# Fused attention and MLP: score pieces regrouped across batches, and pairs released earlier

## The chip, the cores and the metric

The kernel runs on one core of a Trainium2 chip. The metric is the device time of one execution in microseconds (us). A core has a matrix engine (PE, which writes its results to PSUM, eight banks of 128 x 512 float32), a vector engine (DVE), an activation engine (ACT), a general engine (POOL) and a queue for transfers (SP). Each engine works through its own list of instructions in order; semaphores make one wait for another. POOL and ACT can issue transfers as well.

## The reference

For 8 batches of 8 heads with 576 tokens and 64 values per head, attention with 16 extra keys in front ("beacons") that every token sees, then an MLP over all 4608 tokens:

```python
k_all = concat([beacon_k, k]); v_all = concat([beacon_v, v])
scores = (q @ k_all.T) / 8                 # causal among the 576, beacons always seen
a = exp(scores - max); a /= a.sum(-1)
x = (a @ v_all) -> 4608 x 512              # heads side by side
h = relu(x @ w_in) ; out = (h * h) @ w_out # 512 -> 2048 -> 512
```

The kernel computes in bfloat16 with float32 sums and leaves out the maximum.

## The kernel before

**Attention.** The heads are taken two at a time: a pair `p` is 4 x batch + 0..3, so there are 32 pairs. The transposed Q and K of a batch lie in `qT` and `kT`, two buffers each, so batch b uses those of batch b - 2. For batches 0 to 2 the transposes are done on PE; for batches 3 to 7 SP loads float32 tiles into `stg`, POOL casts them into `qk_area`, and SP transposes them by DMA into `qT` and `kT` (`add_trans`, line 543).

The causal scores of a pair have 15 blocks of 128 (or fewer) keys by 128 queries. They are packed into four pieces: three of 512 columns and one, the block of keys 0 to 127 with queries 368 to 495, of 128 columns (`WHOLE`, line 724). A piece is a few score matmuls on PE (line 813), with the two heads of the pair in the two halves of the array's rows, into two PSUM banks. One exponential on ACT (line 830) writes a piece into the pair's buffer `pt`, of which there are four. In batches 1 to 7 the fourth pieces of two pairs share two banks (`SHARED`), so a batch has 14 pieces; each pair still has its own exponential of 2 x 128 values for it. Pieces go to PE in **bursts**: a burst is one planned operation that takes all its banks at once. In batches 2 to 7 the 14 pieces make bursts of 3, 3, 3, 3 and 2 (`SIZES`), and every batch begins anew.

When a pair's exponentials are done, DVE masks the diagonal blocks (lines 848 and 852), PE multiplies with V in an AV group of 30 matmuls (line 869), DVE divides by the sums (lines 884 and 885) into `xn`, and, for batches 1 to 7, SP transposes the five tiles of a batch by DMA into `xT` (line 916), once its four pairs are done.

**MLP.** The tokens are taken in nine chunks of 512. A chunk's first stage (line 997) is 16 groups of 4 matmuls into one bank each, which ACT or DVE empty with the relu (lines 1014 and 1016); DVE squares (line 1023). Its second stage (line 1037) is 64 matmuls. Chunk j needs `xT` of the batches that its tokens lie in, and so the last of the four pairs of those batches.

**What sets the order.** A planner, `Order`, runs when the program is built: it keeps a clock with a duration for each operation, gives each engine the ready operation of the lowest priority number, and the result is written out as each engine's fixed list. Score bursts and AV groups come ahead of the MLP. Two things hold a burst back: its banks (bursts may hold six of the eight; the MLP keeps two) and the **gate** of its first pair (line 768): a pair p of batch 1 or later isn't preferred before the MLP's planned PE time has come to 27.7 x (LEAD + PACE x (p - 4)) us, with 27.7 us a chunk, `LEAD` = -0.4 and `PACE` = 0.25 (line 761). When PE has nothing else, the gate is passed over. The planner takes a transfer as arrived at its reckoned landing and a margin, 2.0 us for the transposes into `qT` and `kT`.

Of the kernel before, what the change touches and what calls it, by code (L numbers as in the profile page):

```python
# [319 lines left out]
def kernel(  # L320
# [29 lines left out]
    def sb(name, shape, dt):  # L350
        return pool.tile(shape, dt, name=name)
# [16 lines left out]
          for i in range(2)]  # L368
    ks = [qk_area[0:NP, (2 * i + 1) * WS:(2 * i + 2) * WS].rearrange("p (h s d) -> p h s d", h=H, s=NS)
          for i in range(2)]  # L370
    bks = sb("bks", [128, H, D], BF16)
    spare = {x: sb(f"spare{x}", [NP, NS * 2 * D], BF16) for x in "kq"}
    vb = [sb(f"vb{i}", [128, NT, H, D + 2], BF16) for i in range(2)]
# [13 lines left out]
    def pair(op, k=0):  # L387
        return ps[:, op.held[k]:op.held[k] + 2, :]
# [12 lines left out]
    def wait_for(later, first):  # L401
# [1 line left out]
            mybir.DependencyClass.Sync, mybir.DependencyReason.DATA), reason="order of loads")  # L403

    order = Order(
        pools={"ps": Banks(), "stg": Slots(NSTG), "pt": Slots(NPT)},
        limits={"late": 4, "strip": 6, "av": 4, "mlp": 4, "tp": 6},
        floors={"mlp": 2},
        keep=2,
# [305 lines left out]
    class Phase:  # L715
# [3 lines left out]
        def __init__(self, pieces, diag, last, tiles, off):  # L719
# [31 lines left out]
    ONE_BY_ONE = [[(x, i)] for x in range(HP) for i in range(4)]  # L751
    SHARED = [[(0, 0)], [(0, 1)], [(0, 2)], [(0, 3), (1, 3)], [(1, 0)], [(1, 1)], [(1, 2)], [(2, 0)], [(2, 1)],
              [(2, 2)], [(2, 3), (3, 3)], [(3, 0)], [(3, 1)], [(3, 2)]]
    PIECES = {b: ONE_BY_ONE if b < 1 else SHARED for b in range(B)}
    SIZES = {b: [2] * 7 if b < 2 else [3, 3, 3, 3, 2] for b in range(B)}

    def phases(b):
        return SPLIT if b < NSPLIT else WHOLE

    mlp_chunk_us = 27.7  # L760
    LEAD, PACE = -0.4, 0.25
    norm_ops = {}

    def add_pair(b, pr):
# [20 lines left out]
    def add_scores(pairs, n, sizes, pieces):  # L785

        work = []
        for shared in pieces:
            at, parts = 0, []
            for x, i in shared:  # L790
                parts.append((pairs[x], i, at, phases(pairs[x].b)[n].pieces[i]))
                at += parts[-1][3][2]
            work.append(parts)
        exps = {x.p: [] for x in pairs}
        at = 0
        for size in sizes:
            group = work[at:at + size]
            at += size
            lead = group[0][0][0]
            prio = 100.0 * lead.p + 1000.0 * n + group[0][0][1]  # L800
            every = [part for parts in group for part in parts]
            cols = sum(t1 - t0 for _, _, _, (mms, _, _) in every for _, t0, t1, _ in mms)
            owners = list({x.p: x for x, _, _, _ in every}.values())
            box = {}

            def emit_qk(e, group=group, box=box):
                for k, parts in enumerate(group):
                    st = pair(box["qk"], k)
                    for x, _, lo, (mms, _, _) in parts:
                        for c, t0, t1, col in mms:  # L810
                            for hj in range(2):
                                hp = slice(64 * hj, 64 * hj + 64)
                                nc.tensor.matmul(  # L813
                                    st[:, hj, lo + col:lo + col + t1 - t0],
                                    kT[x.b % 2][hp, x.pr, 128 * c:128 * c + 128],
                                    qT[x.b % 2][hp, x.pr, t0:t1],
                                    start=True, stop=True,
                                )

            qk = add(f"qk{lead.p}.{n}.{group[0][0][1]}", "PE", cols / 2400.0, emit_qk, prio=prio,  # L820
                     deps=[d for x in owners for d in x.qk_deps + [x.take_pt] + early.get((x.b, x.pr, min(n, 1)), [])],
                     take=("ps", "late" if lead.b < NSPLIT and n else "strip", [2] * size), gate=lead.gate, mode="rows")
            box["qk"] = qk
            for x in owners:
                qk_ops[x.p].append(qk)
            for k, parts in enumerate(group):
                own = []
                for x, i, lo, (_, off, width) in parts:
                    def emit_exp(e, off=off, width=width, k=k, x=x, lo=lo, box=box):
                        nc.scalar.activation(pt[x.take_pt.held[0]][:, :, off:off + width],  # L830
                                             pair(box["qk"], k)[:, :, lo:lo + width], AF.Exp, bias=0.0, scale=scale)

                    own.append(add(f"exp{x.p}.{n}.{i}", "ACT", act(2 * width), emit_exp, prio=prio + 0.1 * k,
                                   deps=[qk], give=(qk, k) if len(parts) == 1 else None))
                    exps[x.p].append(own[-1])
                if len(parts) > 1:
                    add(f"share{lead.p}.{n}.{k}", "-", 0.0, None, deps=own, give=(qk, k))
        assert at == len(work)
        for x in pairs:
            add_phase(x.b, x.pr, x.p, n, phases(x.b)[n], x.take_pt, exps[x.p])  # L840

    def add_phase(b, pr, p, n, ph, take_pt, exps):
        base = 100.0 * p + 1000.0 * n
        def emit_mask(e):
            P = pt[take_pt.held[0]]
            at, step, m0, m = ph.diag
            d = P[:, :, at:at + m * step].rearrange("p h (c w) -> p h c w", w=step)[:, :, :, 0:128]
            nc.vector.tensor_tensor(out=d, in0=d,  # L848
                                    in1=tri[:, m0:m0 + m, :][:, None].to_broadcast([128, 2, m, 128]), op=ALU.min)
            if ph.last is not None:  # L850
                d = P[0:LAST, :, ph.last:ph.last + LAST]
                nc.vector.tensor_tensor(out=d, in0=d,  # L852
                                        in1=tri[0:LAST, 1:2, 0:LAST].to_broadcast([LAST, 2, LAST]), op=ALU.min)

        behind = []
        mask = add(f"mask{p}.{n}", "DVE", 0.08 + 0.15 * ph.diag[3] + (0.26 if ph.last else 0.0), emit_mask,
                   prio=base, deps=exps + (tri_ops[:1] if ph is SPLIT[0] else tri_ops), behind=behind)
        tl, nt = ph.tiles, len(ph.tiles)

        def emit_av(e):  # L860
            P = pt[take_pt.held[0]]
            a = pair(av)
            for hj in range(2):
                h = 2 * pr + hj
                for t in tl:
                    for c in range(t + 1):
                        rr = rows_of(c)
                        o = ph.off[c, t]
                        nc.tensor.matmul(  # L869
                            a[:, hj, (t - tl[0]) * (D + 1):(t - tl[0] + 1) * (D + 1)],  # L870
                            P[0:rr, hj, o:o + 128],
                            vb[b % 2][0:rr, c, h, 0:D + 1],
                            start=(c == 0), stop=(c == t),
                        )

        av = add(f"av{p}.{n}", "PE", 0.0585 * sum(t + 1 for t in tl), emit_av, prio=base + (AVP if ph is SPLIT[0] else -150),
                 deps=[mask] + [cast[b, "v", c] for c in range(tl[-1] + 1)] + av_ops[p], take=("ps", "av", [2]),
                 give=take_pt if ph is phases(b)[-1] else None)
        av_ops[p].append(av)

        def emit_norm(e):
            a = pair(av)[:, :, 0:nt * (D + 1)].rearrange("p h (t d) -> p h t d", d=D + 1)
            r = rcp[(2 * p + n) % len(rcp)][:, :, 0:nt]
            nc.vector.reciprocal(r, a[:, :, :, D])  # L884
            nc.vector.tensor_tensor(  # L885
                out=xn[b % 2].rearrange("p t (h d) -> p h t d", d=D)[:, 2 * pr:2 * pr + 2, tl[0]:tl[0] + nt],
                in0=a[:, :, :, 0:D],
                in1=r[:, :, :, None].to_broadcast([128, 2, nt, D]),
                op=ALU.mult,
            )  # L890

        deps = [av]
        if b >= 2:
            deps += [o for (bb, _), o in xt_ops.items() if bb == b - 2]
        norm_ops[p, n] = add(f"norm{p}.{n}", "DVE", 0.25 + 0.148 * nt, emit_norm, prio=base - 150, deps=deps, give=av)
# [215 lines left out]
    for b in range(B):  # L1111
# [21 lines left out]
        if b < NSPLIT:  # L1133
            for x in pairs:
                for n, ph in enumerate(phases(b)):
                    add_scores([x], n, [1] * len(ph.pieces), [[(0, i)] for i in range(len(ph.pieces))])
        else:
            add_scores(pairs, 0, SIZES[b], PIECES[b])
        if b < NXPE:
            add_xt_pe(b)  # L1140
        else:
            add_xt(b)
        for j in range(NCH):
            if min(((j + 1) * TCH - 1) // S, B - 1) == b:
                late.append(j)
        if b >= 1:
            for j in late:
                add_chunk(j)
            late = []

    turns = TURNS.split()
    named = {o.name: o for o in order.ops}
# [42 lines left out]
```

## Time and profile before

| | us |
|---|---|
| median of 3 runs | 337.4 (337.39 to 338.38) |
| the profiled execution's own time | 337.61 |
| its span, from the first to the last instruction | 335.7 |
| PE busy | 326.6 |
| ACT busy | 194.1 |
| DVE busy | 159.9 |

The busy time of an engine is the time in which at least one of its instructions runs. Matmuls overlap in the array, so lengths of single matmuls add up to more than PE's busy time; distances from start to start are read instead. A line number in a row is that of the kernel before. In rows of the timeline the first number is the start in us from the span's start, the second the time to the end of the last instruction of the run of equal ones, and xN their count. A few matmul records are missing from the trace: a row that shows x7 where the code issues 8 can be such a place.

### The profile page before, as it was taken

What the parts mean: (1) busy time and instruction counts of PE and PEld (TensorE: products, weight loads), DVE (VectorE), ACT (ScalarE), POOL (GpSimd) and SP (SyncE); (2) the same over time, 40 slices, a digit from 0 to 9 for tenths busy, and PEclk for the clock granted to TensorE, in tenths of its full rate; (3) what the DMA queues carried; (4) which work ended last, traced back from release to release, by engine and by line L of the source; (5) the groups of instructions that cost most, each with busy time, mean ns of one, the idle gap of its engine ahead of it and who ended that gap; (6) DMA issues with size and microseconds to landing.
All of it is one profiled execution on the core that took longest, in us unless ns stands there. A gap on an engine that the chain in (4) does not pass through costs nothing.

```text
span 335.7 us, 7764 instructions
## 1 busy us (share of the span) xinstructions
PE 326.6 (97%) x3190; PEld 184.3 (55%) x3231; DVE 159.9 (48%) x329; ACT 194.1 (58%) x296; POOL 84.2 (25%) x130
## 2 busy tenths in 40 slices
PE   7899999999999999999999999999999999999996
PEld 5568765554555455545468945554545444444444
DVE  6689985557423762376136812681258303301400
ACT  3887977577465647574566555665576226515611
POOL 8946504513224332223242240420000000000000
PEclk9999999999999999999999999999999999999999
DMA  8999999899979996899799898973110321011003
GB/s 139 173 204 186 200 205 211 143 235 189 226 113 254 236 213 137 204 232 201 133 253 219 180 182 176 209 155 70 64 64 0 63 71 62 2 62 62 2 5 120
DMA packets 144180, 49.17 MB, mean 146 GB/s; under 512 B 130577, under 2 KB 139665, under 8 KB 144145
## 3 DMA queue, kind: packets, MB, share of 16 engines
q1 hardware_dynamic: 125168, 39.63, 58.2%
q0 software_dynamic: 18624, 8.69, 20.1%
q8 instruction: 25, 0.41, 0.5%
q10 hardware_dynamic: 352, 0.36, 0.4%
q14 instruction: 11, 0.08, 0.1%
HBM read 37.22 MB, written 9.44 MB: 139 GB/s over the span
## 4 chain that ended last, share of the span: by engine, by line
PE 91%; POOL 3%; DMA 3%; issue 1%; DVE 1%; ACT 0%; DVEq 0%
PE ps L997 37%; PE ps L1037 36%; PE ps L869 8%; PE ps L813 8%; DMA w_in<-in_moe_w_in_dram 3%; POOL vb L499 1%; PE ps L671 1%; POOL qk_area L635 1%; PE ps L1080 1%; POOL tri L435 0%; DVE g L1016 0%; POOL w_in L958 0%; DVE tri L414 0%; PE ps L933 0%; POOL vb L498 0%
## 5 line engine op out<-in xcount | busy, mean ns | idle before, releaser
L997 PE MATMUL ps<-xT,w_in 128*128 128x512 bf16 (+3 forms) x688 | 133.7, 340 | 1.2 <-DVE g L1016 0.2
L1037 PE MATMUL ps<-w_out,g 128*128 128x512 bf16 x535 | 125.1, 379 | 1.8 <-issue 0.6
L830 ACT ACTIVATE pt<-ps 128x1024 bf16<-128x1024 f32 (+3 forms) x128 | 103.1, 870 | 28.9 <-PE ps L813 27.8
L997 PEld LDWEIGHTS <-w_in 128*128 128x128 bf16 x704 | 65.5, 98 | 55.5 <-issue 4.1
L1014 ACT ACTIVATE g<-ps 128x512 bf16<-128x512 f32 (+2 forms) x111 | 63.3, 570 | 44.1 <-PE ps L997 43.9
L1037 PEld LDWEIGHTS <-g 128*128 128x128 bf16 x560 | 52.2, 98 | 61.7 <-issue 4.0
L1023 DVE TENSOR_TENSOR g<-g 128x1024 bf16<-128x1024 bf16 (+2 forms) x80 | 51.4, 648 | 65.3 <-ACT g L1014 64.8
L450 ACT COPY osb<-ps 128x512 f32<-128x512 f32 (+2 forms) x37 | 21.3, 576 | 56.7 <-PE ps L1037 43.4
L452 POOL CAST qk_area<-stg 128x512 bf16<-128x512 f32 (+2 forms) x50 | 32.7, 659 | 66.1 <-DMA stg<-in_k_dram 33.2
L848 DVE TENSOR_TENSOR pt<-pt,tri 128x1024 bf16<-128x1024 bf16 (+1 forms) x36 | 23.6, 656 | 40.7 <-ACT pt L830 40.7
L869 PEld LDWEIGHTS <-pt 128*128 128x128 bf16 (+1 forms) x960 | 33.7, 97 | 6.6 <-issue 0.6
L452 POOL CAST vb<-stg 128x512 bf16<-128x512 f32 (+1 forms) x30 | 21.9, 734 | 58.9 <-DMA stg<-in_v_dram 52.9
L1016 DVE TENSOR_SCALAR g<-ps 128x512 bf16<-128x512 f32 (+2 forms) x49 | 28.9, 590 | 15.6 <-PE ps L997 15.3
L869 PE MATMUL ps<-vb,pt 128*128 128x65 bf16 (+1 forms) x960 | 35.0, 193 | 0.3 <-DMA vb<-in_v_dram 0.3
L813 PE MATMUL ps<-qT,kT 64*128 64x80 bf16 (+6 forms) x680 | 32.1, 230 | 0.0
L885 DVE TENSOR_TENSOR xn<-ps,rcp 128x640 bf16<-128x640 f32 (+2 forms) x36 | 27.0, 751 | 1.4
L813 PEld LDWEIGHTS <-kT 64*128 64x128 bf16 x680 | 18.2, 95 | 16.3 <-issue 13.5
L884 DVE RECIPROCAL rcp<-ps 128x10 f32<-128x10 f32 (+2 forms) x36 | 7.6, 211 | 32.6 <-PE ps L869 31.5
L450 ACT COPY qT<-ps 128x576 bf16<-128x576 bf16 (+2 forms) x13 | 7.7, 601 | 4.6 <-PE ps L671 3.3
L452 DVE COPY kT<-ps 128x576 bf16<-128x576 bf16 (+2 forms) x13 | 9.0, 706 | 2.6 <-PE ps L671 2.0
L852 DVE TENSOR_TENSOR pt<-pt,tri 80x160 bf16<-80x160 bf16 x32 | 9.8, 308 | 0.0
L499 POOL DMA_DIRECT2D vb<-in_v_dram x10 | 8.5, 851 | 3.5 <-DMA w_in<-in_moe_w_in_dram 3.1
(54 smaller groups left out, 80.8 us busy)
## 6 DMA issues: line engine op xcount, KB each, us to landing
out_dram<-osb SPq DMA_DIRECT2D x17, 512.0 KB, 3.4
stg<-in_q_dram SPq DMA_DIRECT2D x20, 256.0 KB, 4.8
stg<-in_v_dram SPq DMA_DIRECT2D x18, 256.0 KB, 4.7
stg<-in_k_dram SPq DMA_DIRECT2D x15, 256.0 KB, 4.8
w_in<-in_moe_w_in_dram POOLq DMA_DIRECT2D x4, 512.0 KB, 9.6
w_out<-in_moe_w_out_dram POOLq DMA_DIRECT2D x4, 512.0 KB, 9.8
stg<-in_v_dram SPq DMA_DIRECT2D x6, 224.0 KB, 4.5
qk_area<-in_k_dram POOLq DMA_DIRECT2D x4, 288.0 KB, 12.0
```

Of the source, the lines that this page charges most:

```text
L450: nc.scalar.copy(dst, src)
L452: eng[e].tensor_copy(dst, src)
L813: nc.tensor.matmul(st[:, hj, lo + col:lo + col + t1 - t0], kT[x.b % 2][hp, x.pr, 128 * c:128 * c + 128], qT[x.b % 2][hp, x.pr, t0:t1], sta ...
L830: nc.scalar.activation(pt[x.take_pt.held[0]][:, :, off:off + width], pair(box["qk"], k)[:, :, lo:lo + width], AF.Exp, bias=0.0, scale=scale)
L848: nc.vector.tensor_tensor(out=d, in0=d, in1=tri[:, m0:m0 + m, :][:, None].to_broadcast([128, 2, m, 128]), op=ALU.min)
L869: nc.tensor.matmul(a[:, hj, (t - tl[0]) * (D + 1):(t - tl[0] + 1) * (D + 1)], P[0:rr, hj, o:o + 128], vb[b % 2][0:rr, c, h, 0:D + 1], star ...
L885: nc.vector.tensor_tensor(out=xn[b % 2].rearrange("p t (h d) -> p h t d", d=D)[:, 2 * pr:2 * pr + 2, tl[0]:tl[0] + nt], in0=a[:, :, :, 0:D ...
L997: nc.tensor.matmul(h[:, lo - spans[0][0]:hi - spans[0][0]], w_in_sb[:, mc, ft * 128:(ft + 1) * 128], xT[:, mc, lo % RING:lo % RING + hi - lo],
L1014: nc.scalar.activation(dst, h, AF.Relu, bias=0.0, scale=1.0)
L1016: nc.vector.tensor_scalar(out=dst, in0=h, scalar1=0.0, scalar2=None, op0=ALU.max)
L1023: nc.vector.tensor_tensor(out=d, in0=d, in1=d, op=ALU.mult)
L1037: nc.tensor.matmul(o, G[:, fc, ts * 128:(ts + 1) * 128], w_out_sb[:, fc, :], start=(fc == 0), stop=(fc == NFT - 1))
```

## The change

Four things are changed, all in how score pieces are grouped and when they may start.

1. For batches 3 to 7 the fourth pieces of a batch's four pairs go side by side into one piece of 512 columns. One exponential of 128 x 1024 values empties it into a new buffer `rest` (two of them, in a part of `qk_area` that only batch 1 used before), and the AV groups read that block from there. `rest` is held until the four AV groups of the batch are done.
2. The pieces of batches 3 to 7, 13 a batch, go through one list, `flow`: a batch's shared piece first, then the three large pieces of each pair. A burst takes three from its head, whichever batch they are of, and waits for Q, K and the buffers of all pairs in it; what is left of a batch stays for the next one's pieces. At the end two remain and make the last burst.
3. A pair's mask, AV and normalisation, and a batch's `xT` transposes and MLP chunks, are added when its last piece has gone into a burst; their dependences are the same as before.
4. `LEAD` goes from -0.4 to -1.0, for all pairs from batch 1 on.

A dependence of bursts on `early` is dropped, which for the first phase is in the pairs' own list already.

```diff
+    rest = [qk_area[:, 4 * W + 1024 * i:4 * W + 1024 * (i + 1)].rearrange("p (h w) -> p h w", h=2) for i in range(2)]
...
-        pools={"ps": Banks(), "stg": Slots(NSTG), "pt": Slots(NPT)},
+        pools={"ps": Banks(), "stg": Slots(NSTG), "pt": Slots(NPT), "rest": Slots(2)},
...
-    PIECES = {b: ONE_BY_ONE if b < 1 else SHARED for b in range(B)}
-    SIZES = {b: [2] * 7 if b < 2 else [3, 3, 3, 3, 2] for b in range(B)}
+    PIECES = {0: ONE_BY_ONE, 1: SHARED, 2: SHARED}
+    SIZES = {0: [2] * 7, 1: [2] * 7, 2: [3, 3, 3, 3, 2]}
+    FLOW = 3
...
-    LEAD, PACE = -0.4, 0.25
+    LEAD, PACE = -1.0, 0.25
...
+                def emit_rest(e, k=k, x=x, box=box):
+                    nc.scalar.activation(rest[x.take_rest.held[0]], pair(box["qk"], k), AF.Exp, bias=0.0, scale=scale)
+
+                o = add(f"expr{x.b}", "ACT", act(2 * 512), emit_rest, prio=prio + 0.1 * k, deps=[qk], give=(qk, k))
+                for x, _, _, _ in parts:
+                    exps[x.p].append(o)
...
+    def add_flow(pairs, last):
+        b = pairs[0].b
+        take_rest = add(f"rest{b}", "-", 0.0, None, prio=100.0 * pairs[0].p, deps=pairs[0].qk_deps, take=("rest", "rest", [1]),
+                        gate=pairs[0].gate)
...
+        flow.append([(x, 3, 128 * n, ([(c, t0, t1, 0)], None, 128)) for n, x in enumerate(pairs)])
+        flow.extend([(x, i, 0, pieces[i])] for x in pairs for i in range(3))
+        done = []
+        while len(flow) >= 3 or (last and flow):
+            group = [flow.pop(0) for _ in range(min(3, len(flow)))]
+            add_burst(group, 0, flow_exps)
+            for parts in group:
+                for x, _, _, _ in parts:
+                    flow_left[x.p] -= 1
+                    if not flow_left[x.p]:
+                        add_phase(x.b, x.pr, x.p, 0, phases(x.b)[0], x.take_pt, flow_exps[x.p], x)
+                        if x.pr == HP - 1:
+                            add(f"restg{x.b}", "-", 0.0, None, deps=[o for i in range(HP) for o in av_ops[HP * x.b + i]],
+                                give=x.take_rest)
+                            done.append(x.b)
+        return done
...
+                        keys = P[0:rr, hj, o:o + 128]
+                        if x is not None and (c, t) == (0, 3):
+                            keys = rest[x.take_rest.held[0]][:, hj, 128 * pr:128 * pr + 128]
...
-        else:
+        elif b < FLOW:
             add_scores(pairs, 0, SIZES[b], PIECES[b])
-        if b < NXPE:
-            add_xt_pe(b)
-        else:
-            add_xt(b)
+        for bb in add_flow(pairs, b == B - 1) if b >= FLOW else [b]:
+            if bb < NXPE:
+                add_xt_pe(bb)
+            else:
+                add_xt(bb)
```

`add_burst` is the body of the loop of `add_scores` (lines 799 to 837), now a function that both callers use.

More of the change, by code (lines that the diff above doesn't have):

```diff
@@ L796, in add_scores @@
         for size in sizes:
-            group = work[at:at + size]
+            add_burst(work[at:at + size], n, exps)
             at += size
[L799 to L837, printed above, removed]
@@ L840, in add_scores, with add_burst, emit_qk, emit_exp @@
             add_phase(x.b, x.pr, x.p, n, phases(x.b)[n], x.take_pt, exps[x.p])
-    def add_phase(b, pr, p, n, ph, take_pt, exps):
+    def add_burst(group, n, exps):
+        lead = group[0][0][0]
+        prio = 100.0 * lead.p + 1000.0 * n + group[0][0][1]
+        every = [part for parts in group for part in parts]
+        cols = sum(t1 - t0 for _, _, _, (mms, _, _) in every for _, t0, t1, _ in mms)
+        owners = list({x.p: x for x, _, _, _ in every}.values())
+        slots = [x.take_pt for x, _, _, (_, off, _) in every if off is not None] + [
+            x.take_rest for x, _, _, (_, off, _) in every if off is None]
+        box = {}
+        def emit_qk(e, group=group, box=box):
+            for k, parts in enumerate(group):
+                st = pair(box["qk"], k)
+                for x, _, lo, (mms, _, _) in parts:
+                    for c, t0, t1, col in mms:
+                        for hj in range(2):
+                            hp = slice(64 * hj, 64 * hj + 64)
+                            nc.tensor.matmul(
+                                st[:, hj, lo + col:lo + col + t1 - t0],
+                                kT[x.b % 2][hp, x.pr, 128 * c:128 * c + 128],
+                                qT[x.b % 2][hp, x.pr, t0:t1],
+                                start=True, stop=True,
+                            )
+        qk = add(f"qk{lead.p}.{n}.{group[0][0][1]}", "PE", cols / 2400.0, emit_qk, prio=prio,
+                 deps=[d for x in owners for d in x.qk_deps] + list({id(o): o for o in slots}.values()),
+                 take=("ps", "late" if lead.b < NSPLIT and n else "strip", [2] * len(group)), gate=lead.gate, mode="rows")
+        box["qk"] = qk
+        for x in owners:
+            qk_ops[x.p].append(qk)
+        for k, parts in enumerate(group):
+            own = []
+            if parts[0][3][1] is None:
+                x = parts[0][0]
+                def emit_rest(e, k=k, x=x, box=box):
[3 more added lines that the diff above has]
+                    exps[x.p].append(o)
+                continue
+            for x, i, lo, (_, off, width) in parts:
+                def emit_exp(e, off=off, width=width, k=k, x=x, lo=lo, box=box):
+                    nc.scalar.activation(pt[x.take_pt.held[0]][:, :, off:off + width],
+                                         pair(box["qk"], k)[:, :, lo:lo + width], AF.Exp, bias=0.0, scale=scale)
+                own.append(add(f"exp{x.p}.{n}.{i}", "ACT", act(2 * width), emit_exp, prio=prio + 0.1 * k,
+                               deps=[qk], give=(qk, k) if len(parts) == 1 else None))
+                exps[x.p].append(own[-1])
+            if len(parts) > 1:
+                add(f"share{lead.p}.{n}.{k}", "-", 0.0, None, deps=own, give=(qk, k))
@@ new lines @@
+    flow, flow_exps, flow_left, whole = [], {}, {}, []
+    def add_flow(pairs, last):
+        b = pairs[0].b
+        take_rest = add(f"rest{b}", "-", 0.0, None, prio=100.0 * pairs[0].p, deps=pairs[0].qk_deps, take=("rest", "rest", [1]),
+                        gate=pairs[0].gate)
+        for x in pairs:
+            x.take_rest = take_rest
+            flow_exps[x.p] = []
+            flow_left[x.p] = 4
+        pieces = WHOLE[0].pieces
+        (c, t0, t1, _), = pieces[3][0]
+        flow.append([(x, 3, 128 * n, ([(c, t0, t1, 0)], None, 128)) for n, x in enumerate(pairs)])
[14 more added lines that the diff above has]
+        return done
@@ L843, in add_phase @@
+    def add_phase(b, pr, p, n, ph, take_pt, exps, x=None):
         base = 100.0 * p + 1000.0 * n
@@ L868, in emit_av @@
                         o = ph.off[c, t]
+                        keys = P[0:rr, hj, o:o + 128]
+                        if x is not None and (c, t) == (0, 3):
+                            keys = rest[x.take_rest.held[0]][:, hj, 128 * pr:128 * pr + 128]
                         nc.tensor.matmul(
                             a[:, hj, (t - tl[0]) * (D + 1):(t - tl[0] + 1) * (D + 1)],
-                            P[0:rr, hj, o:o + 128],
+                            keys,
                             vb[b % 2][0:rr, c, h, 0:D + 1],
@@ L1136 @@
                     add_scores([x], n, [1] * len(ph.pieces), [[(0, i)] for i in range(len(ph.pieces))])
-        else:
+        elif b < FLOW:
             add_scores(pairs, 0, SIZES[b], PIECES[b])
-        if b < NXPE:
-            add_xt_pe(b)
-        else:
-            add_xt(b)
[L1143 to L1149, printed above, removed]
+        for bb in add_flow(pairs, b == B - 1) if b >= FLOW else [b]:
[3 more added lines that the diff above has]
+                add_xt(bb)
+            for j in range(NCH):
+                if min(((j + 1) * TCH - 1) // S, B - 1) == bb:
+                    late.append(j)
+            if bb >= 1:
+                for j in late:
+                    add_chunk(j)
+                late = []
     turns = TURNS.split()
```

## The prediction

> **What bounds the kernel now.** I read the page's first two parts, then the waits of PE, then PE's timeline. The page first: engines with their busy time, and the span in 40 slices.
>
> ```profile
> span 335.7 us, 7764 instructions
> PE 326.6 (97%) x3190; PEld 184.3 (55%) x3231; DVE 159.9 (48%) x329; ACT 194.1 (58%) x296; POOL 84.2 (25%) x130
> PE   7899999999999999999999999999999999999996
> PEclk9999999999999999999999999999999999999999
> DMA  8999999899979996899799898973110321011003
> ```
>
> PE is busy in every slice but the first and last few, at the full granted clock; the DMA engines are full as well, but only to slice 27 of 40, some 227 us. Whether PE's busy time hides waiting is told by the view of waits, restricted to PE, from 45 us to the end:
>
> ```profile
> PE ps L1037 <- issue: 0.6, 4, 0.2
> ```
>
> That is its only row: in 291 us PE waits for another engine or a transfer not once that can be seen. So after the start the time is the sum of what stands in PE's queue, and the change can gain only by taking PE time away, and lose only by adding it or by making PE wait. PE's timeline (start, length to the last modelled end, line, count) shows the prices; I read from start to start, since the lengths overlap.
>
> ```profile
> 88.54 1.67 PE L1037 MATMUL ps<-w_out,g 128*128 128x512 bf16 x7
> 90.15 0.84 PE L813 MATMUL ps<-qT,kT 64*128 64x112 bf16 x20
> 90.92 3.63 PE L1037 MATMUL ps<-w_out,g 128*128 128x512 bf16 x16
> 94.48 0.73 PE L813 MATMUL ps<-qT,kT 64*128 64x128 bf16 x20
> 95.37 1.67 PE L1037 MATMUL ps<-w_out,g 128*128 128x512 bf16 x7 [0.16 <-issue]
> ...
> 108.31 0.73 PE L813 MATMUL ps<-qT,kT 64*128 64x256 bf16 x20
> 108.98 3.63 PE L997 MATMUL ps<-xT,w_in 128*128 128x512 bf16 x16
> 112.44 1.07 PE L869 MATMUL ps<-vb,pt 128*128 128x65 bf16 x30
> 113.35 3.62 PE L997 MATMUL ps<-xT,w_in 128*128 128x512 bf16 x15
> 116.90 0.61 PE L813 MATMUL ps<-qT,kT 64*128 64x384 bf16 x8
> 117.45 3.63 PE L997 MATMUL ps<-xT,w_in 128*128 128x512 bf16 x16
> ...
> 125.37 0.84 PE L813 MATMUL ps<-qT,kT 64*128 64x112 bf16 x20
> 126.14 1.04 PE L1037 MATMUL ps<-w_out,g 128*128 128x512 bf16 x4
> ```
>
> Sixteen MLP matmuls ahead of an AV group take 112.44 - 108.98 = 3.46 us (0.216 each); sixteen ahead of a score burst take 94.48 - 90.92 = 3.56. So a burst delays what comes before it by **0.10 us**. The burst at 116.90 takes 0.55 us to the next MLP matmul; its two pieces hold 2 x 512 columns, and two heads run beside each other, so at the MLP's rate they are 2 x 0.216 = 0.43: **0.12 us** more. The one at 125.37 takes 0.77 for three pieces (0.65): 0.12 again. The one at 108.31 takes 0.67 for 2.5 pieces (0.54): 0.13. A burst thus costs its columns plus about 0.22 us, whatever it holds.
>
> As a check, the view of busy time in a stretch, from chunk 1's second stage to the end of chunk 6's first, with all the bursts of batches 3 to 7 in it:
>
> ```profile
> 85.69:263.29 177.60, 175.97 (x1750) 97.55 (x1774) 85.17 (x148) 105.77 (x155) 43.83 (x64) 1.00 0.83 164
> ```
>
> It holds ten half chunks of 64 matmuls (4 x 3.46 = 13.8 each, 138), 25 bursts (per batch 0.77 + 0.67 + 0.77 + 0.55 + 0.67 = 3.43, and five times 0.10: 19.7 in all) and 21 AV groups (113.35 - 112.44 = 0.91, 19.1). That is 176.9 of 177.6 us. At most 0.7 us of it is anything else.
>
> **The change part by part.**
>
> *Fewer bursts.* Before, a batch has 14 pieces in bursts of 3, 3, 3, 3, 2: 25 bursts for five batches. After, it has 13 pieces, and bursts of three run on across batches: 65 pieces make 21 bursts of three and one of two, 22. The matmuls are the same 88 a batch with the same columns (the fourth pieces' 128 columns for four pairs still run two heads abreast). What goes is three times 0.22 = **0.66 us of PE time**, all of it on the path, since PE never waits. Bounds: nothing, if the removed edges come back as waits; and 0.45 a burst by the dearest reading of a row, the burst at 94.48 (0.89 to the next row less 0.54, plus 0.10): 1.35. I don't take that one, because the row after it shows 7 of a group of 8 matmuls, so one matmul's 0.22 is missing from it. [...]
>
> *One exponential for four.* ACT's groups by shape (count, busy, mean ns):
>
> ```profile
> L830 ACT ACTIVATE pt<-ps 128x1024 bf16<-128x1024 f32 x84 | 82.9, 1031 | 18.1 <-PE ps L813 18.1
> L830 ACT ACTIVATE pt<-ps 128x256 bf16<-128x256 f32 x28 | 9.4, 389 | 8.8 <-PE ps L813 8.8
> ```
>
> Per batch four of 389 ns go and one of 1031 comes: 0.53 us less, 2.6 us over five batches, on an engine that is 58% busy and for which PE never waits. Cost and gain 0. The values of a fourth piece now lie in a buffer of their own, free again when the batch's four AV groups are done; with two buffers the next batch finds one free, and the area under them served batch 1 last. 0, bounds 0 and one exponential's 1.0 us a batch on ACT, hidden while PE has MLP work.
>
> *Pairs held across batches.* Batch 3's last piece now shares a burst with batch 4's fourth pieces and the first piece of pair 16, so it waits for batch 4's K; likewise two pieces of batch 4 wait for batch 5's K, and one of batch 6 for batch 7's (batch 5 ends even). So a batch's last AV, its normalisation, its five xT transposes on SP and the MLP chunk behind them hang on the next K transpose. When does that land? SP's transposes into kT for batches 3 to 7, one window each (first and last start; then issue to landing):
>
> ```profile
> L543 SPq DMA_TRANSPOSE kT<-qk_area x1: 3606/3606/3606, 80.8 to 80.8; - x1
> DMA to landing us min/median/max: 5.4/5.4/5.4
> ...
> L543 SPq DMA_TRANSPOSE kT<-qk_area x1: 3174/3174/3174, 115.0 to 115.0; - x1
> DMA to landing us min/median/max: 5.0/5.0/5.0
> ...
> L543 SPq DMA_TRANSPOSE kT<-qk_area x1: 4102/4102/4102, 147.6 to 147.6; - x1
> DMA to landing us min/median/max: 7.7/7.7/7.7
> ...
> L543 SPq DMA_TRANSPOSE kT<-qk_area x1: 4024/4024/4024, 180.4 to 180.4; - x1
> DMA to landing us min/median/max: 5.9/5.9/5.9
> ...
> L543 SPq DMA_TRANSPOSE kT<-qk_area x1: 4212/4212/4212, 217.8 to 217.8; - x1
> DMA to landing us min/median/max: 6.0/6.0/6.0
> ```
>
> K is there at 86.2, 120.0, 155.3, 186.3 and 223.8. The tightest place is chunk 3. Batch 3's last burst now starts at 116.90; with batch 4's K it can start at 120.0, 3.1 us later. The view of xT for that batch and the first use of it on PE:
>
> ```profile
> L916 SPq DMA_TRANSPOSE xT<-xn x5: 1252/1264/1682, 127.3 to 133.0; - x5
> DMA to landing us min/median/max: 2.4/2.5/3.6
> ...
> 137.35 1.03 PE L997 MATMUL ps<-xT,w_in 128*128 128x512 bf16 x4
> ```
>
> Chunk 3 reads tokens up to 2047, so three of the batch's five tiles; the third is issued about 130.2 and lands by 133.8. With 3.1 us more that is 136.9, just ahead of 137.35. And the hole would have a filler: batch 4's bursts, which may now follow at once. I take 0; bounds 0 and 3.1 us.
>
> *Release 0.6 chunk sooner.* A pair p's score bursts are held until the MLP has 27.7 x (lead + 0.25 (p - 4)) us behind it. Pair 12's gate goes from 1.6 chunks (the sixteenth matmul of 128 beyond chunk 1's first half, which is where 90.15 stands) to 1.0. But 0.6 chunk is 16.6 us of MLP, and the K landings above leave only 4.0, 5.4, 5.5, 9.9 and 7.7 us before the first bursts at 90.15, 125.37, 160.78, 196.23 and 231.54 (rows below). So the loads, with the DMA full to some 227 us, become what holds the first burst. No PE work goes or comes: bursts only trade places with MLP matmuls. Batch 2 isn't held by SP's loads and can move up by its whole gate; its five xT transposes (7 to 8 us of SP) may then stand ahead of batch 3's Q and K and push these back, with MLP work of two chunks to cover it.
>
> ```profile
> 160.78 0.84 PE L813 MATMUL ps<-qT,kT 64*128 64x112 bf16 x20
> ...
> 196.23 0.84 PE L813 MATMUL ps<-qT,kT 64*128 64x112 bf16 x20
> ...
> 231.54 0.84 PE L813 MATMUL ps<-qT,kT 64*128 64x112 bf16 x20
> ```
>
> Bursts closer together hold six of eight banks for more of the time, so the MLP works with two. The views of a first stage and a second stage show room for the evictions (stretch, PE, PEld, DVE, ACT busy):
>
> ```profile
> 105.63:120.91 15.28, 15.17 (x117) 7.47 (x118) 9.80 (x17) 10.77 (x17) 4.94 (x6) 1.00 1.17 226
> 120.91:137.35 16.44, 16.17 (x175) 8.54 (x177) 5.54 (x10) 9.28 (x14) 5.43 (x8) 1.00 0.86 164
> ```
>
> Most of the moved bursts of batches 3 to 5 fall into a second stage, where DVE and ACT have 18 of 33 us free. 0; bounds 0 and, if one first-stage tile beside each of the 22 bursts lost a fifth of its 0.86 us (four matmuls), some 3.8 us.
>
> **The sum**: 337.61 (the profiled execution: span 335.7 and 1.9 around it) - 0.66 = 336.95; the median of the runs is 337.4, 0.2 lower, so **336.7**. A measurement of this kernel can tell about 0.3%, 1.0 us, so this counts as no change.
>
> **The rivals.**
>
> *PE waits for K* (the other side). PE's order is written out ahead, by a planner. Now five bursts, the first of batch 3 and those that first touch batches 4, 5, 6 and 7, are meant for the moment when K should land; where it lands later, PE stands, and the MLP matmuls queued behind stand with it. For: equal transposes took 5.0 to 7.7 us, and the present 4 to 10 us of slack go. Against: the planner adds 2.0 us of margin to these transposes (line 551). One place late by the whole spread, or each by a fifth of it, is 2.7: 336.7 + 2.7 = **339.4**. It eats the gain from 0.13 us a place and is slower by 0.3% from 0.33 us a place ((1.0 + 0.66) / 5).
>
> *The MLP runs dry at chunk 3.* For: only 0.4 us left by the working above; against: the filler. Up to 3.1 us: **339.8**.
>
> *More than the edges goes.* A burst's edges at the dear reading (1.35): **336.05**; with the 0.7 us that the check leaves over, 335.4. Against: three burst rows agree on 0.22. [...]
>
> *The release does nothing*, because the loads hold the bursts: the forecast's time, since it counts the release at nothing.
>
> **How the numbers follow.** Forecast 0.56 (0.54 of it within 0.3%, where 336.4 to 338.4 lies, 0.02 beyond it); PE waits for K 0.22 and the MLP dry 0.06, both slower; more than the edges 0.16, nearly all of it faster. So faster 0.17, same 0.56, slower 0.27. The likeliest case alone is 336.4 to 337.4. The range goes down to 336.0 (the dear reading) and up to 339.4 (one whole spread late), which leaves out about 2 in 10.
>
> **What would show it.** Right: 22 groups of score matmuls for batches 3 to 7, edges still 0.10 and 0.12, ACT with five 1024-wide exponentials in place of twenty 256-wide, PE's waits from 45 us on as good as empty, first bursts 4 to 10 us sooner, and the stretch of MLP alone at the end longer by the same. Wrong: a row in PE's waits on SP's transposes into kT or qT (the first rival), on xT before line 997 (the second), or on ACT or DVE before lines 997 and 1037 (the two banks).

## The result, and the profile after

The changed kernel takes 343.0 us (six runs, 341.43 to 343.44) where the kernel before takes 337.39: a ratio of 1.014 (95% interval 1.0118 to 1.0162; the two medians alone divide to 1.017), slower. The profiled execution, at 341.43 us with a span of 339.7, is the quickest of the six.

The same views as of before. In the changed kernel line 826 is the scores, 922 the AV, 1050 and 1090 the MLP's two stages, 969 the xT transposes. The page first:

```profile
span 339.7 us, 7773 instructions
PE 329.8 (97%) x3231; PEld 186.1 (55%) x3231; DVE 156.6 (46%) x320; ACT 198.7 (58%) x290; POOL 87.3 (26%) x130
PE   7999999999999999899999699999999999999996
```

Between start and end PE now has two slices that aren't full, the 17th and the 23rd. The waits of PE from 45 us on, before only 0.6 us of issue, say what they are (engine and line, who ended the wait, us, times, longest):

```profile
PE ps L826 <- DMA kT<-qk_area: 2.7, 1, 2.7
PE ps L1050 <- DMA xT<-xn: 1.6, 1, 1.6
```

PE's timeline around the two, with the wait in brackets, and what each waits for, from the views of SP's transposes into xT and kT there (first and last start; then issue to landing, least, median and most):

```profile
134.78 0.84 PE L826 MATMUL ps<-qT,kT 64*128 64x384 bf16 x20
135.55 1.90 PE L1090 MATMUL ps<-w_out,g 128*128 128x512 bf16 x8
139.03 1.04 PE L1050 MATMUL ps<-xT,w_in 128*128 128x512 bf16 x4 [1.58 <-DMA xT<-xn]
...
185.30 1.91 PE L1050 MATMUL ps<-xT,w_in 128*128 128x256 bf16 x16
189.87 0.84 PE L826 MATMUL ps<-qT,kT 64*128 64x256 bf16 x20 [2.66 <-DMA kT<-qk_area]
190.65 1.59 PE L1050 MATMUL ps<-xT,w_in 128*128 128x256 bf16 x13
```

```profile
L969 SPq DMA_TRANSPOSE xT<-xn x5: 1252/1262/1750, 131.8 to 137.9; - x5
DMA to landing us min/median/max: 2.3/4.1/4.5
...
L544 SPq DMA_TRANSPOSE kT<-qk_area x1: 4069/4069/4069, 182.0 to 182.0; - x1
DMA to landing us min/median/max: 7.9/7.9/7.9
```

The first wait is chunk 3's first stage, waiting for batch 3's xT. The second is a burst that needs batch 6's K: it lands at 182.0 + 7.9 = 189.9, and 2.7 us earlier the matmuls ahead of the burst were done. What stands behind both on PE, MLP work that was ready, waits with them: the eight second-stage matmuls of 139.91 read squares that DVE had finished by 122.3, the first-stage matmuls of 190.65 an xT that had landed by 178.6. The profiled times differ by 341.43 - 337.61 = 3.82 us; the two waits, 4.24, less the 0.66 that was forecast for three bursts' edges make 3.58.

That leaves the step from 341.4 to the usual 343.0. In the profiled execution the mean granted clock was 0.999, with 1.00 in the stretches around both waits (134 to 140 and 186 to 191 us); in the five others it was 0.994 or 0.995, and they took 1.6 us more on average. The experiments below show where that clock goes.

### The profile page after: what moved, and what is told of

It reads as the page before. It is cut to its first block, busy times and chain, and to the rows that moved or that the text cites. A ratio compares the mean times of both kernels' runs of the same rounds, so it can differ in the third digit from the quotient of the medians.

```text
span 339.7 us, 7773 instructions
## 1 busy us (share of the span) xinstructions
PE 329.8 (97%) x3231; PEld 186.1 (55%) x3231; DVE 156.6 (46%) x320; ACT 198.7 (58%) x290; POOL 87.3 (26%) x130
## 4 chain that ended last, share of the span: by engine, by line
PE 88%; DMA 6%; POOL 3%; DVE 1%; SPq 0%; issue 0%; ACT 0%; DVEq 0%
PE ps L1050 36%; PE ps L1090 35%; PE ps L922 8%; PE ps L826 7%; DMA w_in<-in_moe_w_in_dram 3%; DMA kT<-qk_area 2%; DMA xT<-xn 1%; PE ps L672 1%; POOL vb L500 1%; POOL qk_area L636 1%; PE ps L1133 1%; SPq L969 0%; POOL tri L436 0%; DVE g L1069 0%; POOL w_in L1011 0%
## 5 line engine op out<-in xcount | busy, mean ns | idle before, releaser
L1090 PE MATMUL ps<-w_out,g 128*128 128x512 bf16 x560 | 127.9, 379 | 0.0
L853 ACT ACTIVATE pt<-ps 128x1024 bf16<-128x1024 f32 (+4 forms) x108 | 98.3, 956 | 18.1 <-PE ps L826 17.0
L1067 ACT ACTIVATE g<-ps 128x512 bf16<-128x512 f32 (+2 forms) x120 | 68.7, 572 | 43.3 <-PE ps L1050 42.8
L453 POOL CAST qk_area<-stg 128x512 bf16<-128x512 f32 (+2 forms) x50 | 36.1, 728 | 51.1 <-DMA stg<-in_q_dram 26.2
L1069 DVE TENSOR_SCALAR g<-ps 128x512 bf16<-128x512 f32 (+2 forms) x40 | 22.7, 568 | 22.3 <-PE ps L1050 22.1
L902 DVE TENSOR_TENSOR pt<-pt,tri 80x160 bf16<-80x160 bf16 x32 | 12.6, 394 | 0.0
```

The lines of the kernel that those rows point to most:

```text
L453: eng[e].tensor_copy(dst, src)
L1067: nc.scalar.activation(dst, h, AF.Relu, bias=0.0, scale=1.0)
L1069: nc.vector.tensor_scalar(out=dst, in0=h, scalar1=0.0, scalar2=None, op0=ALU.max)
L1090: nc.tensor.matmul(o, G[:, fc, ts * 128:(ts + 1) * 128], w_out_sb[:, fc, :], start=(fc == 0), stop=(fc == NFT - 1))
```

## The experiments

The first four split the change. Theory A blames the bursts across batches, theory B the early release.

**Bursts across batches, released as late as before**, on the changed kernel.

```diff
-    LEAD, PACE = -1.0, 0.25
+    LEAD, PACE = -0.4, 0.25
```

> The changed kernel with the lead back at -0.4: pieces merged and bursts across batches, but pairs released as late as before. Theory A (bursts across batches tie the end of a batch, and with it its xT and the MLP chunk behind it, to the next batch's K): PE's waits stay, now more of them on xT, since the bursts that cross come later still; about 341 to 343 us. Theory B (the early release is to blame: it takes the slack between the landing of K and the first burst): no wait in PE's queue from 45 us on, 22 bursts, 336.7 us.

Measured: 343.38 us, ratio 1.016 (1.0118 to 1.0202). PE waits for xT, as theory A had it. Its timeline at batch 4's xT and chunk 4, and busy times in a stretch that begins within the wait (stretch, PE, PEld, DVE, ACT, POOL; then granted clock, DMA share, GB/s):

```profile
174.33 0.61 PE L826 MATMUL ps<-qT,kT 64*128 64x384 bf16 x8 [0.86 <-DVE xn L938]
174.88 0.61 PE L1050 MATMUL ps<-xT,w_in 128*128 128x256 bf16 x4
179.14 5.66 PE L1050 MATMUL ps<-xT,w_in 128*128 128x256 bf16 x28 [3.66 <-DMA xT<-xn]
```

```profile
177.30:184.20 6.90, 5.06 (x25) 3.59 (x25) 2.13 (x4) 1.19 (x2) 0.00 (x0) 0.51 0.64 153
```

From 177.3 us, 1.8 us before the wait ends, the granted clock is 0.51 for 6.9 us: the 28 matmuls of 256 columns behind it take 5.5 us to the next row's start. At a clock of 1.00 the 16 such matmuls from 190.65 in the changed kernel took 1.75 us to the next row (192.40), 0.11 each, which makes 3.1 for 28.

**The early release alone**, on the kernel before.

```diff
-    LEAD, PACE = -0.4, 0.25
+    LEAD, PACE = -1.0, 0.25
```

> The kernel before with the lead at -1.0 and nothing else: 25 bursts, none of them across batches. Theory A: no wait, or one of under 1 us, on PE from 45 us on; 337 to 338 us. Theory B: PE waits for K transposes (kT) by 2 us and more at one or several batches; 340 to 342 us.

Measured: 342.78 us, ratio 1.0156 (1.0122 to 1.0189), as theory B had it, though mostly by V:

```profile
PE ps L869 <- POOL vb L452: 2.2, 1, 2.2
PE ps L813 <- DMA kT<-qk_area: 1.1, 1, 1.1
PE ps L1037 <- issue: 1.0, 6, 0.2
```

Batch 3's first AV group waits for POOL's cast of a V tile, the batch's last, whose load SP issued at 96.2 us, 4.3 us before the wait ends, and batch 7's first burst waits for K. So each of the two parts costs 1.6% alone, and together they cost no more.

**Merged pieces and the early release, none across batches**, on the changed kernel.

```diff
-        while len(flow) >= 3 or (last and flow):
+        while flow:
```

> The changed kernel with the list of pieces emptied at the end of each batch: fourth pieces merged, lead -1.0, bursts of 3, 3, 3, 3 and 1 per batch, so 25 again and none across batches. Theory A: both waits go; 337 to 338 us, ACT's time like the changed kernel's. Theory B: the wait for K stays, 340 us or more.

Measured: 338.63 us, ratio 1.0038 (1.0017 to 1.006), between the two expectations. The waits of the changed kernel are gone, but another burst waits 1.93 us, for batch 7's K. This profiled execution took 341.69 us with a mean clock of 0.994; the nine others, all at 1.000, 337.8 to 339.3. The busy times around the wait show the difference (columns as above):

```profile
213.00:219.30 6.30, 4.32 (x37) 2.00 (x37) 0.69 (x1) 2.11 (x4) 0.40 (x1) 1.00 1.06 235
219.30:223.20 3.90, 3.90 (x15) 1.12 (x14) 1.48 (x3) 2.81 (x4) 0.61 (x1) 0.57 0.93 184
```

PE stands for 2.0 us and then gets 0.57 of the clock over 3.9 us. That costs 0.43 x 3.9 = 1.7 us, nearly as much again as the wait. The early release alone shows the same step between its executions: 341.93 and 342.09 us at a mean clock of 1.000 and 0.999, 343.46 at 0.995, 344.33 at 0.990. By the clock figures it is also what separates the five slower executions of the changed kernel from its profiled one: a mean clock lower by 0.005 over 341 us is 1.7 us. Those five have no trace, so where in them the clock fell, and after which wait, isn't shown.

**Merged pieces alone.** Both edits above on the changed kernel.

> Fourth pieces merged alone: no bursts across batches, lead -0.4. Both theories: no waits, 25 bursts, so within 0.3% of the kernel before, 337.0 to 337.6 us; were merging itself at fault (ACT or the new buffer), it would be slower by over 1 us.

Measured: 336.99 us, ratio 0.9982 (0.9971 to 0.9993), and PE waits for nobody. Merging is not at fault; it gains a little, 0.5 us. Neither theory holds by itself. Both parts put a burst, an AV group or a first stage right behind an arrival (K, V or xT), and the waits turn up wherever the written order and the arrival miss each other. Theory C: the order isn't bad as such, but the arrivals are later on the chip than the planner reckons.

**The same order, less to load.** Every engine keeps its order, and the transfers get shorter.

```diff
+            hs = slice(0, H // 2) if x == "v" and b >= 3 else slice(0, H)
-            insts.append(queue.dma_start(out=st[lo:rows],
-                                         in_=t[b, :, t0:t0 + rows - lo, :].transpose([1, 0, 2])))
+            insts.append(queue.dma_start(out=st[lo:rows, hs],
+                                         in_=t[b, hs, t0:t0 + rows - lo, :].transpose([1, 0, 2])))
```

> The changed kernel with every engine's order kept, but the V tiles of batches 3 to 7 load only heads 0 to 3 (the other heads are left out: V keeps there whatever the staging buffer held), 2.9 of 17.7 MB of those batches' loads less. Theory C (PE's order is fixed ahead and now asks for K and xT at the moment of their arrival, and the transfers on SP's queue arrive later than that order assumes): both waits of the changed kernel go and the saved burst edges show, 336.7 us. Theory D (the waits come from the order itself, from xT's transposes standing ahead of K's on SP, or from PE's own chain): less traffic changes little, 341 us or more.

> The kernel before with the lead at -1.0, and the same heads of V left out of the loads of batches 3 to 7. Theory C: the waits for V and K go, 337.4 us. Theory D: 341 us or more, as the lead alone gave 342.8.

> The control: the kernel before, with the same heads of V left out of the loads. PE didn't wait there, so both theories give the time of the kernel before, 337.5 us within 0.3%; a gain of over 1 us would say that less traffic speeds up something else too.

Measured, with the kernel before at 337.57 us beside them: the changed kernel 337.03 (0.999, 0.9977 to 1.0003), the early release alone 337.85 (1.0005, 0.9993 to 1.0017), the kernel before 337.66 (1.0009, 0.9994 to 1.0025). The control shows no gain from less traffic where PE didn't wait; both slow kernels lose their 5 to 6 us. In the changed kernel batch 6's K and the burst that waited for it now stand so:

```profile
L545 SPq DMA_TRANSPOSE kT<-qk_area x1: 4557/4557/4557, 176.3 to 176.3; - x1
DMA to landing us min/median/max: 6.3/6.3/6.3
...
185.34 0.84 PE L827 MATMUL ps<-qT,kT 64*128 64x256 bf16 x20
```

K is there at 182.6, 2.7 us ahead of its burst, instead of at 189.9, 2.7 us behind. Theory C stands, theory D falls: every list is as in the changed kernel, and earlier arrivals alone take the waits away. Against the control the changed order is 0.63 us quicker, with intervals that overlap.

**The same transfers, another reckoning.** If arrivals are late against the order, the order can be made for later arrivals.

```diff
-  take=("stg", "stg", [1]), dma=1.2 * max(rows / 128, 0.72) + ...
+  take=("stg", "stg", [1]), dma=1.28 * max(rows / 128, 0.72) + ...
```

> The changed kernel with one number of the planner raised: a load of Q, K or V is reckoned 7% longer (1.28 for 1.2), so PE's order counts on later arrivals; the transfers themselves stay as they are. If only the reckoning was off, the waits go and the saved edges show: 336.7 us. If batch ends that hang on the next batch's K leave PE without MLP work whatever the reckoning, the wait for K goes but PE still waits before chunk 3's first stage (xT or what leads to it), 1 to 3 us, with 338 to 340 us, more where the granted clock falls after it.

> The kernel before with the lead at -1.0 and the loads reckoned 7% longer. If the early release costs only because the order counts on arrivals that come later on the chip, the 5 us that it cost alone go: 337.5 us, no wait for V or K of over 0.5 us. If an early release costs by itself (V and K bunched on SP's queue), 341 us or more.

Measured: the changed kernel 337.28 us, ratio 0.9989 (0.998 to 0.9998); the early release alone 337.33, 0.9995 (0.9983 to 1.0008). One number of the planner takes away the whole loss of either. It moves SP's list as well as PE's: in the changed kernel batch 6's K is now issued at 177.1 us and lands at 184.0, sooner than the 189.9 above, and its burst starts at 191.2, some 4 us later than PE had been ready for it. So these two runs show that another order is enough; that arrivals decide is shown by the runs with less to load. PE's waits from 45 us on are one row in the first and none in the second:

```profile
PE ps L826 <- DVE xn L938: 0.3, 1, 0.3
```

So bursts across batches don't starve the MLP of themselves; I had expected a hole of 1 to 3 us before chunk 3 as one possibility, and there is none.

**The price of a burst.**

```diff
-    SIZES = {b: [2] * 7 if b < 2 else [3, 3, 3, 3, 2] for b in range(B)}
+    SIZES = {b: [2] * 7 if b != 2 else [3, 3, 3, 3, 2] for b in range(B)}
```

> The kernel before with the 14 pieces of batches 3 to 7 in seven bursts of two in place of 3, 3, 3, 3, 2: ten bursts more. [...]

Measured: 339.03 us, ratio 1.0058 (1.0031 to 1.0084). By the ratio that is 0.20 us for each of the ten bursts, with 0.10 to 0.28 as the interval; the prediction's 0.22, 2.2 us for ten, lies in it. By the medians (339.03 against 337.57) it is 0.15. Its timeline shows the edges as read before:

```profile
90.49 1.90 PE L1037 MATMUL ps<-w_out,g 128*128 128x512 bf16 x8
92.32 0.50 PE L813 MATMUL ps<-qT,kT 64*128 64x256 bf16 x8
92.76 3.63 PE L1037 MATMUL ps<-w_out,g 128*128 128x512 bf16 x15
```

Eight MLP matmuls take 1.83 us ahead of the burst, 0.10 over 8 x 0.216; the burst of 1.5 pieces takes 0.44, 0.12 over 1.5 x 0.216.

**Putting it together**, on the changed kernel. Merged pieces, the old lead, bursts across batches where they come late in the kernel, and the longer reckoning.

```diff
-    LEAD, PACE = -1.0, 0.25
+    LEAD, PACE = -0.4, 0.25
...
-        while len(flow) >= 3 or (last and flow):
+        while len(flow) >= 3 or (flow and (last or b < 5)):
...
-  take=("stg", "stg", [1]), dma=1.2 * max(rows / 128, 0.72) + ...
+  take=("stg", "stg", [1]), dma=1.28 * max(rows / 128, 0.72) + ...
```

> Fourth pieces merged, lead back at -0.4, bursts across batches only from batch 5 on (batches 3 and 4 end in a burst of one), and the loads reckoned 7% longer: 23 bursts. If the coupling costs only where K and xT have little slack (batches 3 to 5), no wait appears and two more bursts' edges go than in the merged kernel: 336.6 us. If any crossing costs: a wait at batches 6 or 7 and 338 us or more.

> The merged fourth pieces alone once more (no bursts across batches, lead -0.4), for its small gain: 337.0 us against 337.5 as before, and no wait on PE.

Measured: 336.65 us, ratio 0.997 (0.9958 to 0.9982), 23 bursts and no wait; and merging alone once more 337.2 us, 0.9984 (0.9971 to 0.9996). The first is quicker than both kernels of this case.

## Why the prediction was wrong

- **Fewer bursts, 0.66 us**: the price of a burst roughly holds, at 0.15 to 0.20 us where ten are added; that three fewer give 0.66 isn't shown. Once nothing waits, the changed order is 0.63 us quicker than the kernel before (both with less V to load), but merging alone, which keeps 25 bursts, gains 0.4 and 0.5 us in its two runs. And the changed order with the longer reckoning, 22 bursts and 337.28 us, is no quicker than merging alone beside it, 25 bursts and 337.2.
- **One exponential for four, 0**: right that it costs nothing, and a little too low as a gain. Merging alone is 0.2% quicker in both runs; where that comes from isn't shown.
- **Pairs held across batches, "I take 0; bounds 0 and 3.1 us"**: this step failed. I moved xT by the 3.1 us that batch 4's K comes later than the old last burst, found 0.4 us left, and took batch 4's bursts as a filler for the rest. In the profile batch 3's last burst starts at 120.84, 3.9 us later than before, and DVE has the last of `xn` at 127.3, only 2.4 us later. But SP issued that xT at 131.8, 4.5 us later than before, since its own list, which the term left out, now has three more loads ahead of it. The landings then took 4.1 us in the median where they took 2.5. And PE's list had no filler: the eight ready matmuls of 139.91 didn't pass the first stage that waited ahead of them. PE stood for 1.6 us. SP's rows before, and in the changed kernel:

```profile
121.49 5.72 SPq L513 DMA_DIRECT2D stg<-in_q_dram  x4
127.30 6.91 SPq L916 DMA_TRANSPOSE xT<-xn  x5
...
123.53 5.45 SPq L514 DMA_DIRECT2D stg<-in_q_dram  x4
129.07 1.01 SPq L514 DMA_DIRECT2D stg<-in_k_dram  x1
130.18 0.88 SPq L514 DMA_DIRECT2D stg<-in_q_dram  x1
131.15 0.57 SPq L514 DMA_DIRECT2D stg<-in_k_dram  x1
131.81 7.37 SPq L969 DMA_TRANSPOSE xT<-xn  x5
```

- **Release 0.6 chunk sooner, 0**: this step failed with it. I read that loads would hold the first bursts, and priced that at nothing because bursts "only trade places with MLP matmuls". They do so in the planner's reckoning, not on the chip. With the gate sooner, the 4 to 10 us between K's landing and its burst, which had covered late arrivals of K, were largely gone. Nor did the landings that I read hold for the new order: K of batches 3 to 6 landed 0.7 to 3.6 us later than before, and the first bursts of batches 3 to 7 came 1.6 to 9.3 us sooner, not 4 to 10. A wait for V, the longest of the early release alone, stands in no term. Alone the release cost 1.6%.
- **Bursts closer together, two banks for the MLP, 0**: right. No wait on ACT or DVE before line 1050 or 1090 in the waits above.
- **The rivals.** "PE waits for K" came true at one place, at the 2.7 us that were its price. That the sizes agree is luck: the price was the spread of the landings before (7.7 less 5.0), the wait comes of a landing of 7.9 us, an issue 1.5 us later than before, and a burst for which PE was ready 9 us sooner. "The MLP runs dry at chunk 3" came true with 1.6 of its 3.1 us. Their sum, 341.0, is the profiled execution but for 0.4 us. I gave 0.22 and 0.06 to them as separate cases, though both have one cause, so the range ended at one of them, 339.4. The planner's margin of 2.0 us, which I held against the first, was used up by transfers that ran later than reckoned. Worked out from the changed kernel's code alone, the planner's clock has batch 6's K landing at 180.6 us and its burst starting at 182.8; on the chip PE was ready for that burst at 187.2, 4.4 us later, and K landed at 189.9, 9.3 us later.
- **The clock**: left out. In the profiled executions of two experiments a lower clock cost another 1.7 us on top of a wait of 1.9 or 2.2 us (0.57 of the clock over 3.9 us in one; a mean of 0.995 over 341.7 us in the other). By the clock figures that is the rest of the way to 343.0.

Why batch 6's K in particular was late is argued, not shown: SP issued batch 4's five xT transposes at 168.3 instead of 158.8, just ahead of Q and K of batch 6, as in the rows of SP's timeline below, after the burst that ends batch 4 had waited for batch 5's K (landed at 157.5). The wait is absent without bursts across batches, which fits.

```profile
168.25 7.48 SPq L969 DMA_TRANSPOSE xT<-xn  x5
175.83 0.53 SPq L1115 DMA_DIRECT2D out_dram<-osb  x1
176.47 4.77 SPq L544 DMA_TRANSPOSE qT<-qk_area  x1
181.34 0.54 SPq L1115 DMA_DIRECT2D out_dram<-osb  x1
181.96 4.07 SPq L544 DMA_TRANSPOSE kT<-qk_area  x1
```

## What to carry to other kernels

Where each engine's order is fixed before the run, slack between an arrival and its use is worth what the reckoning of arrivals is off; before it is taken away, compare how late transfers land with what the order counts on, on the chip. A saving of edges that is far smaller than one late arrival (0.66 us against 2.7 here) should come with a mended reckoning, not with less slack. When several rivals share a cause, price them together.

## What the runs showed of the hardware

After a wait of PE of 1.93 us (merged pieces, early release, none across batches) the granted clock was 0.57 over 3.9 us, 1.7 us of loss. After one of 2.15 us (the early release alone, mean clock 0.995) seven second-stage matmuls took 2.64 us to the next row, 101.75 to 104.39, where eight took 1.73 from 105.16 on. With a wait of 3.66 us (bursts across batches, released late) the clock was 0.51 over 6.9 us, from within the wait on. A lower clock didn't follow every wait: the changed kernel's profiled execution stood for 1.58 and 2.66 us with a clock of 1.00 in the stretches around both, while its five other executions had means of 0.994 or 0.995. DMA transposes of one size, those into kT, took from 4.9 to 7.9 us from issue to landing in the kernels before and after; batch 6's took 7.9 us in the changed kernel and 6.3 with less of V to load, and what else moves them isn't shown.
